# A linear-attention and mixture-of-experts kernel: bonus sums in the output's own columns, an earlier state copy, and routing rows copied a chunk later

## The chip, the core and the metric

The kernel runs on one core of one Trainium2 chip. The metric is the device time of one execution in microseconds (us); lower is better. The core's engines work side by side, each through its own list of instructions in a fixed order: PE (TensorE, the matrix engine; its weight loads are shown as PEld), DVE (VectorE), ACT (ScalarE), POOL (GpSimd) and SP (SyncE, which here only issues transfers). They wait for each other through semaphores. PSUM is the memory into which PE writes its products, in banks; SBUF is the large on-chip memory.

## What is computed

Two layers, one after the other. The first is a linear attention with a decaying state, over 4 batches, 8 heads, 768 tokens and a head size of 48:

```python
for t in range(S):
    cur = einsum('bhd,bhe->bhde', u[None] * k[t], v[t])     # the bonus: only for the token itself
    y[:, :, t] = einsum('bhd,bhde->bhe', r[t], state + cur)
    state = w[t][..., None] * state + einsum('bhd,bhe->bhde', k[t], v[t])
```

The second takes y as 3072 tokens x 384 and runs a mixture of experts: a token with `x @ w_skip > 0` goes to the one of 8 experts with the largest `x @ w_gate` and becomes `x + gate * relu(x @ w1[e]) @ w2[e]` (inner size 1024); the others stay as they are.

## The kernel before

The order of the work is written out by hand: each engine gets its instructions in the order in which the program's text issues them, and no scheduler moves them.

**Chunks.** The attention is cut into 24 chunks of 128 tokens (6 for each of 4 batches). For each chunk the decays are turned into running products by scans, so that a chunk becomes a few matrix products. A tile of a chunk has the 8 heads as 4 pairs (index `a`), with the two heads of a pair in the lower and the upper half of the partitions (index `g`).

**The loop.** A loop over `s` from -2 to 24 (L654 to L726) works at several chunks at once. Step `s` does, in the order of the text:

- SP: the loads of chunk s+4 (`wrk`, L164, and the transposed values `vt`) and of the values `vN` of chunk s+3 (L176); in step -2 also a table of constants and the routing weights `wgp_sb` (L172, four transfers). Then, in step -2, ACT copies the odd pairs' routing weights to `wgo_sb` (L665, L666).
- `store(s-1)`: ACT copies the routing logits and the tokens of the chunk before out of PSUM (L471, L474), SP stores them.
- `update(s)`: PE adds k times v of the chunk to the state, which stays in PSUM in the bank `psu` (L415). In the last chunk of a batch DVE zeroes it instead.
- `drip`: one or more routing steps on DVE. When a group of chunks is through, its gates, ranks and one-hot places are worked out by a list of some 25 short steps (they all show line L238, the helper that issues them), which this call hands out one or two at a time between the attention's own steps. Ranks and places are summed by PE in the same PSUM bank as the state.
- `prep_scan(s+2)`: the first scan `q` on DVE (L333), from the products `p` of neighbouring decays, which POOL has made (L317).
- `outputs(s)`: PE adds masked scores times values (L441) and the read of the state copy `sblk` (L447) to y, in the two PSUM banks `psY` (`yb`).
- `prep_keys(s+2)`: POOL scales the keys (`kq`, L349), DVE runs the second scan (L351). `products(s+3)`: POOL makes `p`, `rk` = r times k, and one more (L317, L319, L326).
- `drip` twice; then `prep_reads(s+2)`: DVE scales the reads (`rp`, L356).
- `carry(s)`: DVE decays the state in PSUM (L424). `evict(s)`: ACT copies y to SBUF (`xT`, L453).
- `prep_check(s+2)`: ACT's range check (L364) and a small copy (L366), the last readers of the chunk's `wrk` but for POOL.
- `quadratic(s+1)`: PE's scores (L374), DVE's two masks (L390), then `bonus_sums`: PE sums r u k over each head (L398) into the upper 256 columns of each `psY` bank, and two matmuls of zeros (`warm`, L401) that add nothing to the lower 256 columns, in which y is to be summed; then `keys`: PE transposes the scaled keys (L383) and ACT copies them out (`kt`, L385); then `bonus`: DVE multiplies the sums by the values and writes the product to y's lower columns (L405), to which `outputs` adds in the next step.
- DVE's part of a weight split (L702), `drip` again.
- `carry_out(s)`: ACT copies the decayed state to `sblk` (L433). `rows_out(s)`: PE multiplies `xT` with the routing weights (L461), `wgp_sb` for even pairs and `wgo_sb` for odd ones.
- `flush`: work that the routing has held back for ACT and PE. From step 2 on the weights of the first two experts are loaded and split into high and low halves too, on ACT, POOL and DVE.

**The experts.** Behind the loop the routed tokens are gathered, run through two layers of PE products and scattered. The first expert's tokens come from a gather that starts when all chunks but the last are routed.

A matmul's `start` flag clears what its columns held before; without it the product is added. `QUARTERS` lists the four (`a`, `g`) quarters of each bank with the even `a` first.

## Time and profile before

| | |
|---|---|
| time, median of 3 runs | 314.21 us (312.47 to 315.76) |
| the profiled execution, its own time | 314.95 us |
| its span, first to last instruction | 313.2 us |
| PE busy | 283.3 us (90%) |
| DVE busy | 225.4 us (72%) |
| ACT busy | 157.3 us (50%) |
| POOL busy | 155.3 us (50%) |
| mean granted clock of PE | 0.966 |

The profile has views of one execution: windows give each engine's busy time, PE's granted clock (1.00 is its full speed) and the transfers of a stretch; the timeline gives single instructions in order of time, with the idle time of the engine ahead of them and what ended it; the chain of waits follows the work that ended last back from the end. `psu<-psu,q` means: written psu, read psu and q. A queue's rows (SPq) are its issues, not the transfers themselves. Busy times of an engine's whole span are means over stretches with different limits, so they are read by stretch below.

### The profile page before, as it was taken

The page shows a single profiled execution, that of the slowest core. Times are in us where ns is not written, and L with a number is a line of the kernel's source. Part 1 is how long each engine was busy: PE and PEld are TensorE (multiplying, and loading weights), DVE is VectorE, ACT ScalarE, POOL GpSimd, SP SyncE. Part 2 cuts the span into 40 slices and gives each one's busy share as a digit, 9 for nine tenths or more (in the row PEclk, how much of TensorE's full clock was granted, in tenths as well). Part 3 has the DMA queues.
Part 4 walks back from the last instruction along what each step waited for, and adds up shares of the span by engine and source line. Part 5 has one row for each costly group of instructions (what it writes and reads, how often), then busy time and mean ns, then how long its engine had stood idle before and what let it go on. Part 6 is the DMA issues. An engine that isn't in the chain of part 4 may idle for free.

```text
span 313.2 us, 9163 instructions
## 1 busy us (share of the span) xinstructions
PE 283.3 (90%) x3642; PEld 260.0 (83%) x3642; DVE 225.4 (72%) x482; ACT 157.3 (50%) x419; POOL 155.3 (50%) x157
## 2 busy tenths in 40 slices
PE   8629999699899799989788999999999999999992
PEld 3328888688788688778688899999999999999992
DVE  5755979979999999998435579496785859496320
ACT  2035555448956478649122458184664828184200
POOL 4976998678998879973103314231222222101111
PEclk9978999879999999999969999999999999999999
DMA  6949999999999998863121196847576474750001
GB/s 149 246 111 256 233 285 245 259 285 295 255 284 277 299 258 224 217 214 96 30 72 40 63 287 246 274 174 251 222 253 235 166 265 157 244 170 27 6 2 39
DMA packets 25604, 60.37 MB, mean 193 GB/s; under 512 B 4326, under 2 KB 15562, under 8 KB 25552
## 3 DMA queue, kind: packets, MB, share of 16 engines
q1 hardware_dynamic: 23184, 53.70, 59.4%
q0 software_dynamic: 2048, 5.48, 5.6%
q10 hardware_dynamic: 320, 0.53, 0.8%
q8 instruction: 30, 0.49, 0.7%
q14 instruction: 22, 0.18, 0.2%
HBM read 52.64 MB, written 7.86 MB: 193 GB/s over the span
## 4 chain that ended last, share of the span: by engine, by line
PE 73%; DMA 9%; ACT 5%; issue 5%; DVE 5%; POOL 1%; POOLq 0%; DVEq 0%; ACTq 0%; SPq 0%
PE psO L860 7%; PE psO L862 7%; PE psO L861 7%; PE psH L839 6%; PE psH L838 6%; PE psH L837 6%; PE psY L441 6%; PE psA L374 5%; PE psH L128 4%; PE psY L398 3%; PE psX L461 3%; PE psY L447 3%; PE psu L415 3%; DMA vt<-wrk 3%; PE psY L401 2%
## 5 line engine op out<-in xcount | busy, mean ns | idle before, releaser
L801 POOL DMA_INDIRECT out<-fin,ids x16 | 16.8, 1051 | 79.3 <-DVE fin L867 44.5
L844 ACT ACTIVATE hh<-psH 128x256 fp32r<-128x256 f32 x60 | 23.1, 384 | 57.9 <-PE psH L839 53.8
L839 PE MATMUL psH<-xTh,w1l 128*128 128x256 f32 x168 | 47.5, 283 | 0.0
L838 PE MATMUL psH<-xTl,w1h 128*128 128x256 f32 x168 | 47.5, 283 | 0.0
L837 PE MATMUL psH<-xTh,w1h 128*128 128x256 f32 x168 | 47.5, 283 | 0.0
L860 PE MATMUL psO<-w2h,hh 128*128 128x384 f32 x120 | 40.8, 340 | 0.0
L862 PE MATMUL psO<-w2h,hl 128*128 128x384 f32 x120 | 40.2, 335 | 0.0
L861 PE MATMUL psO<-w2l,hh 128*128 128x384 f32 x120 | 40.1, 334 | 0.0
L326 POOL TENSOR_TENSOR wrk<-wrk 128x512 f32<-128x512 f32 x24 | 36.5, 1521 | 1.8
L736 POOL DMA_INDIRECT xg<-out,idr x15 | 17.1, 1140 | 40.2 <-DMA out<-fin,ids 25.1
L390 DVE TENSOR_TENSOR asb<-psA,c_sb 128x512 f32<-128x512 f32 x48 | 30.8, 682 | 7.8 <-PE psA L374 7.5
L845 DVE SCALAR_TENSOR_TENSOR hl<-psH,hh 128x256 fp32r<-128x256 f32 x60 | 25.2, 420 | 13.3 <-ACT hh L844 13.0
L349 POOL TENSOR_TENSOR kq<-wrk,q 128x512 f32<-128x512 f32 x24 | 26.9, 1119 | 11.3 <-DVE q L333 10.9
L839 PEld LDWEIGHTS psH<-xTh,w1l 128*128 128x128 f32 x168 | 32.2, 192 | 0.0
L838 PEld LDWEIGHTS psH<-xTl,w1h 128*128 128x128 f32 x168 | 32.2, 192 | 0.0
L837 PEld LDWEIGHTS psH<-xTh,w1h 128*128 128x128 f32 x168 | 32.2, 191 | 0.0
L867 DVE SCALAR_TENSOR_TENSOR fin<-psO,gates,xg 128x384 f32<-128x384 f32 x15 | 9.3, 618 | 28.5 <-PE psO L862 28.5
L441 PE MATMUL psY<-asb,vN 128*64 128x128 f32 (+1 forms) x384 | 27.6, 290 | 2.2 <-DVE psY L405 2.2
L374 PE MATMUL psA<-rp,kq 64*64 64x128 f32 (+1 forms) x768 | 27.5, 261 | 2.2 <-POOL kq L349 2.2
L319 POOL TENSOR_TENSOR rk<-wrk 128x512 f32<-128x512 f32 x23 | 29.3, 1274 | 0.0
L98 DVE TENSOR_TENSOR w2l<-r,w2h 128x512 fp32r<-128x512 f32 x42 | 27.8, 687 | 1.0
L453 ACT COPY xT<-psY 128x512 f32<-128x512 f32 x24 | 14.0, 582 | 27.7 <-PE psY L447 20.2
(155 smaller groups left out, 686.9 us busy)
## 6 DMA issues: line engine op xcount, KB each, us to landing
r<-w SPq DMA_DIRECT2D x48, 512.0 KB, 5.8
wrk<-wrk SPq DMA_DIRECT2D x23, 577.9 KB, 8.1
vN<-vN SPq DMA_DIRECT2D x24, 192.0 KB, 4.7
out<-x SPq DMA_DIRECT2D x24, 192.0 KB, 5.8
vt<-wrk SPq DMA_DIRECT2D x24, 96.0 KB, 5.7
vt<-wrk SPq DMA_DIRECT2D x48, 48.0 KB, 5.3
out<-fin,ids POOLq DMA_INDIRECT x16, 4.7
xg<-out,idr POOLq DMA_INDIRECT x15, 3.9
```

What stands on the lines that cost most here:

```text
L98: (eng or nc.vector).tensor_tensor(dst_l, src, dst_h.bitcast(F32), op=ALU.subtract)
L319: (nc.gpsimd if i else nc.vector).tensor_tensor(rk.rearrange("p a j -> p (a j)"), t[:, R_OFF:K_OFF], t[:, K_OFF:V_OFF], op=ALU.mult)
L326: nc.gpsimd.tensor_tensor(rk1, rk1, two(1, 1, CW), op=ALU.mult)
L374: nc.tensor.matmul(psa[g][j:j + HP, a, j:], wk["kq"][rows, a, j:j + HP], wk["rp"][rows, a, j:], start=True, stop=True)
L390: nc.vector.tensor_tensor(s, psa[g], tri.rearrange("p (o j) -> p o j", o=1).to_broadcast([P, NP, P]), op=ALU.mult)
L441: nc.tensor.matmul(quarter(0, a, g, w), head(i, 2 * a + g, w), wk["asb"][g][:, a], start=False, stop=(c == 0), skip_group_check=True)
L837: nc.tensor.matmul(ps, w1h[:, o:o + P], xTh[:, kc], start=(kc == 0), stop=False)
L838: nc.tensor.matmul(ps, w1h[:, o:o + P], xTl[:, kc], start=False, stop=False)
L839: nc.tensor.matmul(ps, w1l[:, o:o + P], xTh[:, kc], start=False, stop=(kc == KC - 1))
L860: nc.tensor.matmul(pso, h[j, fc][0], w2h[:, o], start=(fc == 0), stop=False)
L861: nc.tensor.matmul(pso, h[j, fc][0], w2l[:, o], start=False, stop=False)
L862: nc.tensor.matmul(pso, h[j, fc][1], w2h[:, o], start=False, stop=(fc == FC - 1))
```

## The change

Three things are edited.

1. `bonus_sums` writes into y's own 256 columns of each bank, not into the upper ones, and `bonus` multiplies there in place. Only the matmuls with an even `a` carry the `start` flag. The two zero matmuls (L401) go. `keys` is issued ahead of `bonus_sums`.
2. `carry` and `carry_out` are issued directly behind `prep_keys` and `products`: on DVE the decay stands ahead of the two routing steps and of `rp`, and on ACT the state copy stands ahead of the eviction and the check.
3. The two copies into `wgo_sb` are issued in step 0 behind `quadratic(1)`, not in step -2.

```diff
--- before.py
+++ after.py
@@ -285,8 +285,8 @@
             scores(i)
             mask(i, 0)
             mask(i, 1)
+            keys(i)
             bonus_sums(i)
-            keys(i)
             bonus(i)
 
         later, held, rare = deque(), [], []
@@ -395,14 +395,11 @@
         def bonus_sums(i):
             for a, g in QUARTERS:
                 rows = slice(64 * g, 64 * g + HP)
-                nc.tensor.matmul(quarter(2 * P, a, g, HP), ubk_sb[rows, a], work[i]["rk"][rows, a],
-                                 start=True, stop=True, skip_group_check=True)
-            for h in range(2):
-                nc.tensor.matmul(yb[:, h, :2 * P], warm[:, :P], warm[:, :2 * P],
-                                 start=False, stop=True, skip_group_check=True)
+                nc.tensor.matmul(quarter(0, a, g, HP), ubk_sb[rows, a], work[i]["rk"][rows, a],
+                                 start=(a % 2 == 0), stop=True, skip_group_check=True)
 
         def bonus(i):
-            nc.vector.tensor_tensor(yb[:, :, :2 * P], yb[:, :, 2 * P:],
+            nc.vector.tensor_tensor(yb[:, :, :2 * P], yb[:, :, :2 * P],
                                     ab(vt_sb[i % (NBUF + 1)]), op=ALU.mult)
 
         def update(i):
@@ -662,8 +659,6 @@
                     for h in range(2):
                         hs = slice(2 * h, 2 * h + 2)
                         halves(nc.sync, wgp_sb[:, hs], wgp[:, hs], swap=bool(h))
-                    nc.scalar.copy(wgo_sb[:, :, E + 1:], wgp_sb[:, 1::2, :2 * D])
-                    nc.scalar.copy(wgo_sb[:, :, :E + 1], wgp_sb[:, 1::2, 2 * D:])
                 if s == -1:
                     nc.sync.dma_start(wgs_sb, wgs)
                 if on(s - 1):
@@ -688,10 +683,13 @@
                     prep_keys(s + 2)
                     if on(s + 3):
                         products(s + 3)
+                if on(s):
+                    carry(s)
+                    carry_out(s)
+                if on(s + 2):
                     drip(2 * pace[0])
                     prep_reads(s + 2)
                 if on(s):
-                    carry(s)
                     evict(s)
                 if on(s + 2):
                     prep_check(s + 2)
@@ -701,10 +699,11 @@
                     if lows and s % 2:
                         nc.vector.tensor_tensor(*lows.pop(0), op=ALU.subtract)
                     drip(2 * pace[0])
-                if on(s):
-                    carry_out(s)
                 if s == n - 1:
                     early_tokens(0)
+                if s == 0:
+                    nc.scalar.copy(wgo_sb[:, :, E + 1:], wgp_sb[:, 1::2, :2 * D])
+                    nc.scalar.copy(wgo_sb[:, :, :E + 1], wgp_sb[:, 1::2, 2 * D:])
                 if on(s):
                     rows_out(s)
                 flush()
```

**ACT, at the program's start.** The kernel before, from the copy of the bonus vector on (`junk` with `wrk` is the range check, `kt` the key copy, `xT` the eviction, `sblk` the state copy):

```order
L267 COPY ubk_sb<-u_sb 128x256
L665 COPY wgo_sb<-wgp_sb 128x2x96
L666 COPY wgo_sb<-wgp_sb 128x2x9
L364 ACTIVATE junk_233,viol<-wrk_82,bias_lo 128x512
L366 COPY q0all<-q_220 128x4
L385 COPY kt_280<-psT_275 128x512
L364 ACTIVATE junk_294,viol<-wrk_83,bias_lo 128x512
L366 COPY q0all<-q_243 128x4
L453 COPY xT_332<-psY 128x512
L364 ACTIVATE junk_334,viol<-wrk_84,bias_lo 128x512
```

The changed kernel, from the same place:

```order
L267 COPY ubk_sb<-u_sb 128x256
L364 ACTIVATE junk_231,viol<-wrk_82,bias_lo 128x512
L366 COPY q0all<-q_218 128x4
L385 COPY kt_268<-psT_263 128x512
L364 ACTIVATE junk_290,viol<-wrk_83,bias_lo 128x512
L366 COPY q0all<-q_241 128x4
L430 COPY sblk_117<-psu 128x4x48
L450 COPY xT_329<-psY 128x512
L364 ACTIVATE junk_331,viol<-wrk_84,bias_lo 128x512
L366 COPY q0all<-q_306 128x4
L385 COPY kt_359<-psT_354 128x512
L705 COPY wgo_sb<-wgp_sb 128x2x96
```

The two routing-row copies have moved from ahead of the first check to behind the second key copy, and the first state copy stands ahead of the first eviction, where it came three instructions later.

**PE, in an early chunk**, from the bonus sums to the routing rows (`rk` against `ubk_sb` are the bonus sums, `kq` the key transposes). Before:

```order
L398 MATMUL psY<-rk_289,ubk_sb 64x128 x8
L401 LDWEIGHTS warm
L401 MATMUL psY<-warm 128x256
L401 LDWEIGHTS warm
L401 MATMUL psY<-warm 128x256
L383 MATMUL psT_465<-c_sb,kq_321 128x128 x4
L461 MATMUL psX_474<-wgp_sb,xT_430 128x105
```

And now:

```order
L383 MATMUL psT_452<-c_sb,kq_317 128x128 x4
L398 MATMUL psY<-rk_285,ubk_sb 64x128 x8
L458 MATMUL psX_468<-wgp_sb,xT_427 128x105
L458 MATMUL psX_468<-wgo_sb,xT_427 128x105
L458 MATMUL psX_468<-wgp_sb,xT_427 128x105
```

The key transposes have moved ahead of the bonus sums, and the two zero matmuls with their weight loads are gone.

**DVE, in one later chunk with routing steps** (L238; `oh` is a one-hot compare, `MEMSET psu` zeroes the ranks' columns of the state's bank), from the first scan to the masks. Before:

```order
L333 SCALAR_TENSOR_TENSOR q_1633<-p_1543,pss 128x260
L346 RECIPROCAL p_1543<-q_1633 128x4
L351 SCALAR_TENSOR_TENSOR pss<-p_1543,pss 128x260
L238 TENSOR_TENSOR oh_1660<-key,pss 128x48
L238 MEMSET psu 128x48
L356 TENSOR_TENSOR rp_1663<-wrk_82,pss 128x512
L424 TENSOR_TENSOR psu<-psu,q_1529 128x4x48
L390 TENSOR_TENSOR asb_14_1687<-psA_114,c_sb 128x512
```

And now:

```order
L333 SCALAR_TENSOR_TENSOR q_1605<-p_1517,pss 128x260
L346 RECIPROCAL p_1517<-q_1605 128x4
L351 SCALAR_TENSOR_TENSOR pss<-p_1517,pss 128x260
L421 TENSOR_TENSOR psu<-psu,q_1503 128x4x48
L238 TENSOR_TENSOR oh_1634<-key,pss 128x48
L238 MEMSET psu 128x48
L356 TENSOR_TENSOR rp_1637<-wrk_82,pss 128x512
L390 TENSOR_TENSOR asb_14_1660<-psA_114,c_sb 128x512
```

The decay of the state (L424 before, L421 now) has moved from behind `rp` to directly behind the second scan, ahead of both routing steps.

## Rows read from the trace of the kernel before

**Rows 1.** Windows: stretch, length, busy us (count) PE, PEld, DVE, ACT, POOL; PE clock, DMA share, GB/s.

```profile
20.50:46.60 26.10, 25.32 (x512) 22.56 (x516) 20.05 (x38) 13.53 (x44) 20.75 (x21) 0.90 0.96 248
46.60:141.00 94.40, 85.04 (x1721) 74.18 (x1714) 87.51 (x190) 59.21 (x180) 80.58 (x74) 0.96 0.96 259
...
200.00:250.00 50.00, 50.00 (x363) 50.00 (x363) 36.81 (x69) 29.95 (x66) 12.90 (x12) 1.00 0.63 213
```

**Rows 2.** Timeline, start of ACT and PE: start, duration, engine, line, op, [idle before, releaser].

```profile
19.39 0.35 ACT L665 COPY wgo_sb<-wgp_sb 128x192 f32<-128x192 f32 x1 [11.59 <-DMA wgp_sb<-wgp]
...
19.76 0.72 ACT L364 ACTIVATE junk<-wrk,bias_lo 128x512 bf16<-128x512 f32 x1
...
20.56 0.58 ACT L385 COPY kt<-psT 128x512 f32<-128x512 f32 x1
...
21.19 1.09 PE L415 MATMUL psu<-vN,kt 128*64 128x48 f32 x16 [6.20 <-ACT kt L385]
```

**Rows 3.** Timeline, from the start to the second eviction: SP, POOL, DVE, PE, ACT.

```profile
13.26 3.07 SPq L172 DMA_DIRECT2D wgp_sb<-wgp  x4
...
17.19 0.62 POOL L317 TENSOR_TENSOR p<-wrk 128x260 f32<-128x260 f32 x1
...
20.64 0.31 SPq L164 DMA_DIRECT2D wrk<-wrk  x1
20.76 0.69 DVE L333 TENSOR_TENSOR_SCAN q<-p,pss 128x260 f32<-128x260 f32 x1 [3.41 <-ACT q0all L366]
...
21.70 0.70 DVE L351 TENSOR_TENSOR_SCAN pss<-p,pss 128x260 f32<-128x260 f32 x1
...
25.77 0.62 POOL L317 TENSOR_TENSOR p<-wrk 128x260 f32<-128x260 f32 x1 [3.02 <-DMA wrk<-wrk]
...
26.93 0.37 PE L461 MATMUL psX<-wgp_sb,xT 128*128 128x105 f32 x2
...
30.20 0.59 ACT L453 COPY xT<-psY 128x512 f32<-128x512 f32 x1 [1.58 <-PE psY L447]
```

**Rows 4.** Windows on either side of two falls of PE's clock.

```profile
57.50:60.00 2.50, 0.47 (x6) 0.30 (x6) 2.34 (x7) 0.69 (x4) 2.50 (x3) 0.98 1.07 286
60.00:61.30 1.30, 0.96 (x17) 0.80 (x18) 1.30 (x4) 0.97 (x4) 1.22 (x2) 0.50 1.04 207
...
21.20:25.80 4.60, 4.60 (x72) 4.27 (x76) 2.10 (x5) 2.13 (x7) 1.15 (x2) 0.51 0.97 241
12.20:19.00 6.80, 2.29 (x54) 1.87 (x54) 3.96 (x7) 0.00 (x0) 6.64 (x7) 0.99 0.72 168
```

**Rows 5.** Chain of waits, one early chunk: start, us, engine, tile, line.

```profile
38.35 0.67 PE psu L415 x16
...
41.87 0.33 PE psY L401 x2
...
43.53 0.67 PE psu L415 x16
```

**Rows 6.** Timeline of the same early chunk, DVE and ACT.

```profile
38.98 0.70 DVE L351 TENSOR_TENSOR_SCAN pss<-p,pss 128x260 f32<-128x260 f32 x1
...
39.77 0.69 DVE L356 TENSOR_TENSOR rp<-wrk,pss 128x512 f32<-128x512 f32 x1
...
40.38 0.36 DVE L424 TENSOR_TENSOR psu<-psu,q 128x192 f32<-128x192 f32 x1
...
43.16 0.32 ACT L433 COPY sblk<-psu 128x192 f32<-128x192 f32 x1
```

**Rows 7.** Timeline of loaded chunks: waits of DVE, ACT and PE.

```profile
66.60 1.29 DVE L390 TENSOR_TENSOR asb<-psA,c_sb 128x512 f32<-128x512 f32 x2 [1.56 <-PE psA L374]
...
108.11 0.32 ACT L433 COPY sblk<-psu 128x192 f32<-128x192 f32 x1 [2.06 <-DVE rnk L238]
...
108.48 0.67 PE L415 MATMUL psu<-vN,kt 128*64 128x48 f32 x16 [2.18 <-ACT sblk L433]
...
111.56 1.29 DVE L390 TENSOR_TENSOR asb<-psA,c_sb 128x512 f32<-128x512 f32 x2 [0.40 <-PE psA L374]
```

## The prediction

> **What bounds the kernel now.** I read the windows first, to see which engine is full in which stretch, then the timeline of the start, of one early chunk and of the chunks where an engine sat idle over a releaser, and the chain of waits for what one chunk costs on PE. Three regimes come out. In the expert phase PE is busy 50.00 of 50.00 us [rows 1], and nothing of the change is in it, so it can only move earlier as a block. In the early chunks (20.5 to 46.6) PE is busy 25.32 of 26.10 us, DVE 20.05: PE sets the pace. In the loaded chunks (46.6 to 141), where weight splits and routing steps are added, DVE is busy 87.51 of 94.40 us [rows 1]: all its idle time is 6.9 us, the ceiling for any gain there that comes from order alone.
>
> The start is a wait by itself. ACT stands 11.59 us in front of the routing-row copy (L665), whose input lands at about 19.3; behind it in ACT's order are the check of chunk 0 (L364) and the copy of chunk 0's keys (L385), and PE, free since 14.99, waits 6.20 us for the latter [rows 2].
>
> **The start, part by part.** With L665 and L666 gone from the front, the keys (done by 14.99) are copied by 14.99 + 0.58 = 15.6, and PE's first state update is 5.5 us earlier than its 21.19 [rows 2]. That much doesn't last, because the decay and the state copy now stand ahead of the eviction on ACT. For chunk 0: p of chunk 2 ends at 17.19 + 0.62 = 17.8; from q to the end of the second scan takes 22.40 - 20.76 = 1.64, so 19.5 [rows 3]; decay 0.36 and state copy 0.32 [rows 6]: 20.2; eviction 0.59 [rows 3]: 20.8; the check 0.80 (19.76 to 20.56), the next key copy 0.58 and the two routing-row copies 0.37 (19.39 to 19.76) [rows 2]: 22.6. Only then can PE run the routing rows of chunk 0 to their end, which it began at 26.93 [rows 3]: 4.3 us earlier, and the second eviction with them (30.20 becomes 25.9). The load of chunk 3 must keep up: it went out at 20.64 and landed 5.13 later, at 25.77 [rows 3]. Its release on ACT is the check of chunk 0, no longer held; ahead of it on SP stand the four issues that end at 13.26 + 3.07 = 16.3 [rows 3]. It has to go out by about 17.7 (25.9 less 0.4 for copy and hand-over, 0.36, 1.64, 0.7 for p and hand-over, 5.13), so it just does.
>
> Against this stands PE's clock. It was granted 0.99 until 19.0 and half (1.2 of 2.4 GHz) until 25.8; in the stretch before the fall PE was busy 2.29 of 6.80 us, and before the later fall at 60.0 it was busy 0.47 of 2.50 [rows 4]. The 30.20 already contains 4.60 us of PE work at half rate, about 2.3 us. In the changed kernel PE still idles from the keys of chunk 1 (about 18.9) until 20.8, and again until about 22.6, so I expect a fall once more, now over a stretch that is nearly all work: a loss of 1.9 us (if it begins in that idle time) to 3.4 (half of 6.8). I take 3.0. **Start: 4.3 - 3.0 = 1.3 saved**, bounds 0.9 and 4.3.
>
> **The zero matmuls.** Two of 128x256 a chunk, 48 in all, go; the chain of waits puts them at 0.33 us [rows 5]. In the early chunks, 5.18 apart (38.35 to 43.53) [rows 5], the state copy ended at 43.16 + 0.32 [rows 6], just ahead of the next update at 43.53: PE and ACT are tied there, and removing the matmuls alone would gain little more than the tie allows. The new order unties them: the copy moves up, the keys stand ahead of the sums, and the eviction, which the sums now wait for as before, is covered by scores and keys. So 0.33 for three chunks until DVE takes over: **1.0 saved**, bounds 0.3 (one chunk) and 1.7 (five). In the loaded chunks it is idle time of PE, worth nothing by itself.
>
> **The decay ahead of rp.** No instruction is added or removed on DVE. Now rp waits for the scan just before it: start to start 0.79 (38.98 to 39.77), where the decay follows rp after 0.61 (39.77 to 40.38) [rows 6]. With the decay between them the 0.18 is covered; I take 0.15 for the 8 of 14 loaded chunks with a decay where no routing step already fills it: **1.2 saved**, bounds 0 and 2.5 (0.18 for all 14). The early state copy also ends waits such as ACT's 2.06 us for a routing step, after which PE waited 2.18 and DVE 0.40 for the scores [rows 7]: of these only DVE's 0.4 is time. **0.4 saved**, bounds 0 and 1. New on DVE is that a routing memset of the bank stands two places behind the decay in one chunk and waits there for ACT's copy, with rp, masks and the bonus product queued behind it and PE's outputs waiting for those: **0.3 lost** (0.32 plus hand-over, less one short step), bound 1.
>
> What hides the later eviction: the decay waits for DVE's scan, so in loaded chunks the eviction comes up to 1.3 us later than PE is done. Scan to sums' end is 0.6 + 0.36 + 0.32 + 0.59 + 0.67, 2.5 us; DVE's own way from the scan to the bonus product is decay, rp and two masks, 0.6 + 0.3 + 0.6 + 1.2 = 2.7 [rows 6, 7] (0.67 taken as for the update [rows 5]). It fits by 0.2. Without that margin, every chunk pays the excess.
>
> Last, PE idles 0.33 us more in each loaded chunk, and a fall of its clock there costs DVE a wait like the 1.56 us for scores at 66.60 [rows 7], with hand-overs 1.9. I charge a fifth of one: **0.4 lost**.
>
> **Sum**: 1.3 + 1.0 + 1.2 + 0.4 - 0.3 - 0.4 = 3.2 us. The profiled execution took 314.95 us (313.2 of span, 1.75 around it) and gives 311.75; it lies 0.74 above the median of the runs, 314.21, from which I count: **311.0**. A measurement here tells about 1% (3.1 us) from no change.
>
> **A rule weighed.** The 2.06 us in [rows 7] is ACT waiting for a DVE step that only reads the bank it reads itself. The Trainium skill (PSUM — Partial Sum Buffer, PSUM bank collisions raise a hardware error) says that any two engines on one bank and quadrant must be kept apart, reads against reads included; the trace agrees. By the rule alone the waits would only turn round: the routing steps that touch the bank (four memsets and four rank products) would wait for the copy.
>
> **Rivals.**
> - *No fall at the start.* PE keeps full rate: 3.0 more, 308.0. For it: two idle stretches with work between them are not one of 6.20. Against it: the fall at 60.0 followed 2.0 us of idle PE. Chance 0.14.
> - *More falls later.* PE loses the filler and its clock falls once or twice more between 70 and 141, each 1.9: 312.9 to 314.8, taken as 313.5. PE was idle 9.4 of 94.4 us there [rows 1] and would be idle some 15. The Trainium skill (TensorE: Matmul & The Clock Gate, Part 1) calls the throttled state the default, which activity releases; the falls in [rows 4] agree. Chance 0.18.
> - *Waits turned round.* All eight routing steps, not one, pay 0.3 behind the copy: 311.0 + 7 x 0.3 = 313.1. This is what the rule on banks would do here; the order shows only one so close. Chance 0.06.
> - *Transfers keep the lead.* Queues were busy 0.96 over the loaded chunks at 259 GB/s [rows 1]; if loads and not DVE set the pace there, the 1.3 and 1.0 are given back: 313.3. Against it, DVE's 93%. Chance 0.08.
> - *Slower: the eviction behind the decay.* If in loaded chunks ACT reaches the state copy late (it also holds one-hot rows and weight casts), sums and bonus product come late, DVE waits and every chunk lengthens. Below 0.2 us a chunk nothing happens; above it 14 chunks pay: from 0.65 us of delay, (0.65 - 0.2) x 14 = 6.3, it is slower by over 1%: 317.4. Chance 0.07.
> - The forecast, 309.5 to 312.5 by itself: 0.47.
>
> Faster by over 1% (under 311.07): half of the forecast's 0.47, the 0.14 of the first rival, and little of the rest (0.04): 0.42. Slower: 0.07. Within 1%: 0.51. The range leaves out the far half of the first rival, below 307.5, and the last one: 307.5 to 314.5.
>
> **What would show it.** Right: ACT's key copy near 15, PE's first update before 16, the second eviction near 26 (full clock) or near 28 (half); early chunks 4.85 apart; state copy directly after the decay, no wait of it for a routing step. Wrong: evictions that wait for the state copy while DVE waits for the sums; a new half-clock stretch between 70 and 141; p waiting for loads. If the start alone gives more than 3 us, the fall was mis-sized.

## The result and the profile after

The changed kernel takes 311.83 us (median of 20 runs, 309.92 to 315.20) where the kernel before takes 315.74 (20 runs); the ratio is 0.9892, with a 95% interval from 0.9859 to 0.9925. That is 3.4 us less by the ratio. The forecast was 3.2 us less and 311.0 us. Executions of one kernel differ by 2 to 3%, and a profile shows one execution; so times of the whole are taken from the ratios below, and the profiles tell where they come from. A ratio compares those runs of each kernel that lie within 1.5% of its fastest, which are 19 of the changed kernel's 20, but only 2 of 12 for E6 below and 3 of 6 for E12.

The profiled execution of the changed kernel has a span of 308.5 us, 4.7 less than before. The first two windows of [rows 1], of the changed kernel:

```profile
20.50:46.60 26.10, 25.09 (x484) 21.36 (x488) 21.21 (x41) 13.80 (x45) 23.00 (x22) 0.93 0.99 260
46.60:141.00 94.40, 84.18 (x1703) 71.02 (x1695) 87.60 (x192) 60.72 (x181) 81.19 (x75) 0.98 0.93 249
```

The regimes are what they were: DVE is busy 87.60 of 94.40 us in the loaded chunks, where it was 87.51. No sum of busy times shows a gain. The gain shows when the same points of the program are set side by side (starts in the two profiled executions; the gather is the first expert's, on POOL):

| stretch | before | after | difference | forecast |
|---|---|---|---|---|
| start to the second eviction | 30.20 | 26.75 | -3.45 | -1.3 |
| second to sixth eviction (chunks 1 to 5) | 20.11 | 20.17 | +0.06 | -1.0 |
| sixth eviction to the gather's issue | 104.28 | 104.89 | +0.61 | -0.9 |
| gather's issue to the end | 158.57 | 156.72 | -1.9 | 0 |

So the total came out as forecast, and no line of the sum did. Both columns are one execution each, and the one of before is not a firm base: E2 and E3 below, in which the routing-row copies stand where they stood before, have their second eviction at 28.34 and 29.38, with PE's clock falling at 16.5 and 18.2 and not at 18.9. At most 0.7 us of E2's 1.9 are its own zero matmuls of two chunks. The experiments ask where the gain comes from.

ACT in the changed kernel, timeline of the start, to set beside [rows 2, 3]:

```profile
14.19 0.58 ACT L385 COPY kt<-psT 128x512 f32<-128x512 f32 x1 [5.04 <-PE psT L383]
...
19.60 0.32 ACT L430 COPY sblk<-psu 128x192 f32<-128x192 f32 x1 [4.03 <-DVE psu L421]
19.81 0.59 ACT L450 COPY xT<-psY 128x512 f32<-128x512 f32 x1
...
21.57 0.37 ACT L705 COPY wgo_sb<-wgp_sb 128x192 f32<-128x192 f32 x1
...
26.75 0.58 ACT L450 COPY xT<-psY 128x512 f32<-128x512 f32 x1 [1.56 <-PE psY L444]
```

The wait of 11.59 us for the routing rows is gone and the keys are copied at 14.19. ACT's wait is now 4.03 us for DVE's decay, and the first eviction, whose input PE had long finished, stands behind it.

PE of the changed kernel, from chunk 0's outputs to the routing rows, timeline and then windows (columns as in [rows 1]):

```profile
18.29 0.66 PE L383 MATMUL psT<-c_sb,kq 128*128 128x128 f32 x4
20.46 0.67 PE L398 MATMUL psY<-rk,ubk_sb 64*64 64x128 f32 x16 [1.51 <-ACT xT L450]
...
22.10 0.47 PE L458 MATMUL psX<-wgo_sb,xT 128*128 128x105 f32 x2 [0.58 <-ACT wgo_sb L706]
```

```profile
18.95:20.40 1.45, 0.00 (x0) 0.00 (x0) 0.56 (x2) 0.80 (x3) 1.42 (x1) 1.00 0.80 185
...
22.10:22.60 0.50, 0.50 (x4) 0.50 (x5) 0.50 (x2) 0.00 (x0) 0.50 (x2) 0.88 1.04 358
...
23.30:25.70 2.40, 2.40 (x31) 2.37 (x32) 2.08 (x5) 0.94 (x4) 2.24 (x3) 0.50 1.09 248
```

PE waits 1.51 us for the eviction and 0.58 for the routing rows, as forecast; its clock stays at 1.00 through the first wait and falls only at about 22.5. The half-rate stretch covers 3.2 us of work, not 6.8.

### The profile page after: what moved, and what is told of

It is laid out like the page before. It is cut to its first block, busy times and chain, and to the rows that moved or that the text cites. A ratio compares the mean times of both kernels' runs of the same rounds, so it can differ in the third digit from the quotient of the medians.

```text
span 308.5 us, 9037 instructions
## 1 busy us (share of the span) xinstructions
PE 281.7 (91%) x3594; PEld 254.1 (82%) x3594; DVE 225.3 (73%) x482; ACT 157.8 (51%) x419; POOL 155.8 (50%) x157
## 4 chain that ended last, share of the span: by engine, by line
PE 68%; DVE 13%; issue 6%; DMA 4%; POOL 3%; ACT 3%; POOLq 0%; DVEq 0%; ACTq 0%; SPq 0%
PE psO L861 7%; PE psO L859 7%; PE psO L860 7%; PE psH L838 7%; PE psH L837 7%; PE psH L836 7%; PE psY L438 4%; PE psX L458 4%; PE psA L374 4%; PE psY L398 4%; PE psH L128 3%; PE psY L444 2%; PE psT L383 2%; PE psu L412 2%; DVE q L333 2%
## 5 line engine op out<-in xcount | busy, mean ns | idle before, releaser
L735 POOL DMA_INDIRECT xg<-out,idr x15 | 16.4, 1096 | 36.0 <-DMA out<-fin,ids 22.4
L349 POOL TENSOR_TENSOR kq<-wrk,q 128x512 f32<-128x512 f32 x24 | 26.9, 1119 | 11.6 <-DVE q L333 10.3
L374 PE MATMUL psA<-rp,kq 64*64 64x128 f32 (+1 forms) x768 | 25.9, 251 | 3.3 <-POOL kq L349 1.9
L98 DVE TENSOR_TENSOR w1l<-r,w1h 128x512 fp32r<-128x512 f32 x36 | 24.9, 693 | 2.1
```

What stands on the lines that cost most here:

```text
L98: (eng or nc.vector).tensor_tensor(dst_l, src, dst_h.bitcast(F32), op=ALU.subtract)
L374: nc.tensor.matmul(psa[g][j:j + HP, a, j:], wk["kq"][rows, a, j:j + HP], wk["rp"][rows, a, j:], start=True, stop=True)
```

## The experiments

In the table, "second eviction" and "lead" (how much earlier than in the kernel before chunk 5 is evicted) come from the profiled execution. So do the next four columns, for the stretch of the loaded chunks from chunk 7's first scan to chunk 23's second mask: its length, DVE's busy time in it (overlaps counted once), what DVE's six weight-split subtractions took (five of them lie in that stretch in E5), and DVE's idle time, which is the rest. The last column is how long POOL's product `p` waited for a chunk's load between 46.6 and 141 us of the same execution.

| kernel | ratio to before (95%) | second eviction | lead | loaded | DVE busy | splits | DVE idle | POOL waits for loads |
|---|---|---|---|---|---|---|---|---|
| before | 1 | 30.20 | 0 | 104.0 | 94.0 | 6.95 | 10.0 | 0.5 |
| after | 0.989 (0.986 to 0.993) | 26.75 | 3.4 | 104.6 | 94.2 | 7.11 | 10.5 | 3.0 |
| E1 copies alone | 0.992 (0.987 to 0.997) | 25.49 | 4.45 | 104.05 | 94.1 | 7.07 | 9.9 | 0.2 |
| E2 bonus sums alone | 1.005 (1.001 to 1.010) | 28.34 | 1.7 | 106.9 | 95.5 | 7.99 | 11.5 | 8.1 |
| E3 early carry alone | 1.007 (1.003 to 1.011) | 29.38 | 1.1 | 106.5 | 95.9 | 8.61 | 10.7 | 0 |
| E4 after, sums first | 1.003 (0.998 to 1.008) | 28.54 | 2.3 | 106.6 | 96.8 | 9.43 | 9.8 | 6.1 |
| E5 after, splits ahead of the scan | 0.985 (0.977 to 0.993) | 25.42 | 4.7 | 103.9 | 91.95 | 4.02 | 12.0 | 0 |
| E6 after, eviction first | 0.984 (0.976 to 0.993) | 25.75 | 3.8 | 108.05 | 96.7 | 8.94 | 11.4 | 4.8 |
| E7 after, splits on POOL | 0.988 (0.981 to 0.996) | 26.98 | 3.2 | 101.8 | 86.7 | none | 15.1 | 0.9 |
| E8 = E4 + E6 + E7 | 0.986 (0.981 to 0.991) | 26.46 | 4.1 | 104.2 | 87.9 | none | 16.3 | 2.5 |
| E9 after, zeros at the start | 0.989 (0.982 to 0.996) | 25.57 | 3.7 | 106.6 | 95.0 | 8.27 | 11.6 | 6.9 |
| E10 = E8 + E9 | 0.990 (0.985 to 0.995) | 24.76 | 5.0 | 106.8 | 87.5 | none | 19.3 | 5.0 |
| E11 = E1 + splits on POOL | 0.997 (0.992 to 1.003) | 26.80 | 2.7 | 107.1 | 89.1 | none | 18.0 | 3.5 |
| E12 = E4 + E6, splits a step later | 0.980 (0.972 to 0.989) | 24.84 | 3.3 | 107.5 | 93.5 | 8.03 | 14.0 | 8.6 |

### E1: the routing-row copies alone

```diff
 # the kernel before; in step -2, behind the loads of wgp_sb
-                    nc.scalar.copy(wgo_sb[:, :, E + 1:], wgp_sb[:, 1::2, :2 * D])
-                    nc.scalar.copy(wgo_sb[:, :, :E + 1], wgp_sb[:, 1::2, 2 * D:])
 # in step 0, ahead of rows_out
+                    nc.scalar.copy(wgo_sb[:, :, E + 1:], wgp_sb[:, 1::2, :2 * D])
+                    nc.scalar.copy(wgo_sb[:, :, :E + 1], wgp_sb[:, 1::2, 2 * D:])
```

> The kernel before with part 3 alone: the two routing-row copies (L665, L666 of before) behind quadratic(1) in step 0, all else as before. Theory (nearly all that the change gains is gained at the start): the key copy near 14.2 us, the first update near 14.8, the second eviction at 26.8 us or earlier, since here the first eviction stands ahead of the decay and not behind it; later chunks keep that lead, and the ratio to the kernel before is 0.986 to 0.990. Rival (the prediction's own sum: the start is worth 1.3 us and the other two parts the rest): ratio 0.995 to 0.997.

ACT's timeline of the start:

```profile
15.02 0.58 ACT L385 COPY kt<-psT 128x512 f32<-128x512 f32 x1 [5.66 <-PE psT L383]
...
17.26 0.59 ACT L453 COPY xT<-psY 128x512 f32<-128x512 f32 x1 [0.86 <-PE psY L441]
...
25.49 0.58 ACT L453 COPY xT<-psY 128x512 f32<-128x512 f32 x1 [1.49 <-PE psY L447]
```

The first eviction is at 17.26 where the changed kernel has 19.81, and the second at 25.49. Behind that, each of chunks 3 to 22 is evicted 4.34 to 4.45 us earlier than before: the old schedule, moved as a block. In this execution the copies alone give more than the whole change does. The trace is the theory's; the ratio, 0.992, lies between the theory's range and the rival's, and its interval reaches into both. It can't be told apart from the whole change's 0.989.

### E2 and E4: the zero matmuls and the order of keys and sums

```diff
 # E2: the kernel before
-                nc.tensor.matmul(quarter(2 * P, a, g, HP), ubk_sb[rows, a], work[i]["rk"][rows, a],
-                                 start=True, stop=True, skip_group_check=True)
-            for h in range(2):
-                nc.tensor.matmul(yb[:, h, :2 * P], warm[:, :P], warm[:, :2 * P],
-                                 start=False, stop=True, skip_group_check=True)
+                nc.tensor.matmul(quarter(0, a, g, HP), ubk_sb[rows, a], work[i]["rk"][rows, a],
+                                 start=(a % 2 == 0), stop=True, skip_group_check=True)
...
 # E4: the changed kernel
-            keys(i)
             bonus_sums(i)
+            keys(i)
```

> The kernel before with part 1 alone and with the sums still ahead of the key transposes: bonus sums in y's own columns, one start flag per bank, no zero matmuls, keys behind the sums. Theory (the 0.33 us of the two zero matmuls was eaten by PE's changes between products of 64x64 and of 128x128 weights, each 0.17 us of PE time, of which the new order has two more): with one such change as before, early chunks come 4.85 us apart, where they were 5.18 before and are 5.20 in the changed kernel. Rival (something else holds the early chunks at 5.2, such as POOL, busy 18.63 of 20.10 us there, or sums that write where y is evicted from): 5.1 to 5.2. The start is as before, second eviction near 30.2; total 0.5 to 1.3 us less by the theory, none by the rival.

> The changed kernel with the bonus sums ahead of the key transposes again, as before the change; all else changed. Theory (changes between 64x64 and 128x128 weights cost 0.17 us of PE time each, and the order keys, sums, rows has two more of them): early chunks 4.85 us apart and not 5.20, 1.0 us gained by chunk 5 and kept or lost to DVE's pace later: 0 to 1.2 us under the changed kernel, ratio 0.985 to 0.989 to the kernel before. Rival (the keys stand ahead to cover the wait of the sums for the eviction, so without them PE waits for ACT): a wait of PE at the sums for the eviction of 0.2 us or more in each early chunk, 5.1 to 5.4 apart, ratio 0.989 to 0.995.

What led to them is PE's part in an early chunk, which has no gap in either kernel. The chain of waits, before and then after (start, us, engine, tile, line):

```profile
36.19 0.51 PE psY L398 x16
36.69 0.32 PE psY L401 x2
37.02 0.44 PE psT L383 x4
37.45 0.87 PE psX L461 x8
```

```profile
37.95 0.59 PE psT L383 x4
38.54 0.60 PE psY L398 x16
39.14 1.07 PE psX L458 x8
40.21 0.60 PE psu L412 x16
```

Sums, zeros, keys and rows took 2.14 us; without the zeros, keys, sums and rows take 2.26. The weight loads of the changed kernel (timeline, PEld) say why:

```profile
37.88 0.43 PEld L383 LDWEIGHTS psT<-c_sb,kq 128*128 128x128 f32 x4 [0.17 <-issue]
38.47 0.43 PEld L398 LDWEIGHTS psY<-rk,ubk_sb 64*64 64x64 f32 x16 [0.16 <-ACT junk L364]
39.07 0.30 PEld L458 LDWEIGHTS psX<-wgp_sb,xT 128*128 128x128 f32 x2 [0.17 <-issue]
```

In front of each of them stand 0.16 to 0.17 us in which nothing is waited for that explains it (ACT's check, named in the second row, ended 0.02 us before it, but the same 0.17 us stand in front of the sums at 102.14, where the last check ended 5.7 us earlier), and each is a change between weights of 64x64 and of 128x128. The order scores, sums, zeros, keys, rows had one such change; scores, keys, sums, rows has three. The Trainium skill (TensorEngine Tiling (Array Packing), Tiling Modes) says that a change of the tiling mode drains the engine. The trace agrees, with about 0.17 us a change. With the sums first again, E4's evictions in early chunks (ACT, timeline):

```profile
38.53 0.58 ACT L450 COPY xT<-psY 128x512 f32<-128x512 f32 x1 [0.18 <-PE psY L444]
...
43.45 0.58 ACT L450 COPY xT<-psY 128x512 f32<-128x512 f32 x1
```

They are 4.92 apart, where the changed kernel has 5.20, no wait for the eviction of 0.2 us stands in each chunk, and of the three gaps one is left: the theory holds. E2 has 5.01 to 5.06 up to chunk 4, less than before but not 4.85. A weight load of PE waits there for the late state copy (0.19 us at 36.14), the tie that the prediction had seen.

Yet the total of E4 is 1.003 and that of E2 1.005, where both theories had a gain. What is won in the early chunks is lost in the loaded ones, which E5 to E7 take up. The starts of these two executions were the clock's: in E4 it was at half from 20.8 to 27.6, with the second eviction at 28.54; in E2 it fell early, and the eviction came at 28.34 where its theory had 30.2.

### E3: decay and state copy early, alone

```diff
 # the kernel before, with the order of the changed one
+                    carry(s); carry_out(s)          # behind prep_keys and products
                     drip(2 * pace[0])
                     prep_reads(s + 2)
-                    carry(s)
                     evict(s)
...
-                    carry_out(s)
```

> The kernel before with part 2 alone: decay and state copy directly behind prep_keys and products, ahead of routing steps, rp and eviction. Theory (this part gives nothing in the loaded chunks: DVE was idle 6.9 us there before and is idle 7.3 us in the changed kernel, its waits only stand elsewhere): from the eviction of chunk 5 to the gather's issue within 0.8 us of before's 104.28, ratio 0.998 to 1.003; the eviction of chunk 6, which comes behind the state copy, later by some 3 us and caught up by chunk 7. Rival (the prediction's: 0.9 us saved): ratio 0.997, and 103.4 between the two.

The ratio is 1.007 and the stretch from chunk 5 to the gather 106.9 us: a loss, beyond both theories (and by the windows above DVE is idle 6.8 us in the changed kernel, not the theory's 7.3). Chunk 6 is evicted 7.95 us behind chunk 5, as in the changed kernel, and what the two kernels share there is seen in the changed one (timeline of ACT, then PE):

```profile
54.65 0.32 ACT L430 COPY sblk<-psu 128x192 f32<-128x192 f32 x1 [4.02 <-DVE psu L421]
54.86 0.59 ACT L450 COPY xT<-psY 128x512 f32<-128x512 f32 x1
```

```profile
55.51 0.67 PE L398 MATMUL psY<-rk,ubk_sb 64*64 64x128 f32 x16 [2.45 <-ACT xT L450]
```

DVE is late with the decay, the eviction waits behind the copy and PE waits 2.45 us for it. Between 46.6 and 141 us the changed kernel has seven such waits (in total, times, longest); the kernel before has four of 1.8 us in all:

```profile
PE psY L398 <- ACT xT L450: 7.9, 7, 2.4
```

Behind the wait in chunk 6 PE's clock falls, and DVE waits for PE twice (windows, then DVE's timeline, of the changed kernel):

```profile
56.60:60.00 3.40, 3.40 (x36) 3.21 (x37) 2.57 (x9) 1.40 (x6) 1.85 (x2) 0.50 1.00 288
```

```profile
58.84 0.10 DVE L238 MEMSET psu<- 128x48 f32 x1 [0.69 <-PE psu L412]
...
61.20 0.37 DVE L421 TENSOR_TENSOR psu<-psu,q 128x192 f32<-128x192 f32 x1 [0.76 <-PE psu L510]
```

So the next chunk has not quite caught up: chunk 7 is evicted 2.6 us ahead of the kernel before, where chunk 5 was 3.4 ahead. The kernel before pays for such a fall too, at 59.9 ([rows 4]), with waits of DVE of 0.30 and 1.56 us. In E3 DVE waits 1.58 us at a routing step's memset for PE's state update, its six splits take 8.61 us instead of 6.95, and chunk 7 is 0.3 us behind the kernel before, where chunk 5 was 1.1 ahead.

### E5, E6 and E7: what DVE and POOL do to each other, and the order on ACT

```diff
 # E5: the changed kernel; ahead of the scan of an odd chunk, no longer behind the bonus product
+            if lows and i % 2:
+                nc.vector.tensor_tensor(*lows.pop(0), op=ALU.subtract)
...
 # E6: the changed kernel
-                    carry_out(s)
...
                     evict(s)
+                    carry_out(s)
...
 # E7: the changed kernel; POOL takes a split at every step, DVE none
-            if lows and i % 2 == 0:
+            if lows:
                 nc.gpsimd.tensor_tensor(*lows.pop(0), op=ALU.subtract)
```

> The changed kernel with DVE's six weight-split subtractions (L700) moved from behind the bonus product to directly ahead of the next odd chunk's first scan, where POOL has run out of work or is about to. Theory (a DVE operation with all operands in SBUF stands still while POOL works through an operation of its own, so the loaded chunks are as long as these meetings make them): the six take under 6 us in all, where they take 7.1 us in the changed kernel, 6.95 before and 9.4 with the sums first (0.68 each alone), and the stretch from the eviction of chunk 5 to the gather's issue is 1 to 2 us under the 104.9 us of the changed kernel. Rival (the loaded chunks' length is set by loads or by waits of DVE, not by these meetings): the six get shorter or not, and the stretch stays within 0.7 us of 104.9.

> The changed kernel with the state copy (L430) behind the eviction on ACT again; the decay stays early on DVE. Theory (at the start, and in chunk 6, the first of a batch, the eviction waits for nothing but the decay that stands ahead of the copy): first eviction at 17.3 us and not 19.8, second at 25.5 and not 26.8, chunk 6 evicted 4.5 us behind chunk 5 and not 7.95; lead of about 4.4 us over the kernel before at chunk 5, where the changed kernel has 3.4. In total 0 to 1.5 us under the changed kernel. Rival (the copy ahead of the eviction pays, since the next chunk's state read hangs on it): early chunks more than 5.25 apart, and no gain.

> The changed kernel with the six weight-split subtractions of DVE (L700) given to POOL, ahead of its key product in the odd chunks, as POOL has six in the even ones. Theory (DVE sets the pace of the loaded chunks, 7.1 us of it are these six and more is lost to their meetings with POOL's operations; POOL was busy 81 of 94 us and takes six of 1.3 to 1.7 us): loaded chunks shorter by 2 to 4 us in all until POOL is full too, ratio to the kernel before 0.977 to 0.985. Rival (POOL becomes the bound, or the loads are): loaded chunks as long as in the changed kernel, within 0.7 us, and DVE idle in front of masks or rp.

What lengthens the splits was read from DVE's and POOL's timelines side by side. One split of the kernel before, then one of E4 with what POOL did meanwhile:

```profile
68.40 0.68 DVE L702 TENSOR_TENSOR w2l<-r,w2h 128x512 fp32r<-128x512 f32 x1
```

```profile
122.98 1.98 DVE L700 TENSOR_TENSOR w1l<-r,w1h 128x512 fp32r<-128x512 f32 x1
124.89 0.68 DVE L333 TENSOR_TENSOR_SCAN q<-p,pss 128x260 f32<-128x260 f32 x1
...
122.91 1.51 POOL L326 TENSOR_TENSOR wrk<-wrk 128x512 f32<-128x512 f32 x1
124.49 1.60 POOL L331 TENSOR_TENSOR w1l<-r,w1h 128x512 fp32r<-128x512 f32 x1
```

Alone, the subtraction takes 0.68 us. Started 0.07 us behind one of POOL's products it takes 1.98 and ends 0.5 us behind that product's end, and POOL's next one takes 1.60 where its shortest took 1.26. DVE's other work on 128x512 (masks, bonus product, reads) has an operand in PSUM and stays at 0.67 to 0.72 in all kernels. The pattern holds for all 60 splits that DVE makes in the ten kernels where it makes any: the 51 that started while one of POOL's operations had more than 0.04 us to go ended 0.54 to 0.55 us behind that operation's end, whatever they took (0.73 to 2.04 us); the other nine took 0.68 to 0.69. The Trainium skill (SBUF — State Buffer, Who interferes with whom) says that a DVE instruction with two inputs in SBUF contends with a GpSimd instruction that reads SBUF, for a pair of ports that only one of them can hold; the traces agree, with these 51 and nine. The profile counts such a wait as busy time, which is why "DVE is busy 93%" looked like work.

So what the splits take is set by where they fall among POOL's operations, and every edit ahead of them can shift that. It is not shown that the length of the loaded chunks follows from it. Set against the kernel before, E4's loaded chunks are 2.6 us longer and DVE's busy time there 2.8 us more. But E2's and E9's are 2.9 and 2.6 us longer with only 1.4 and 1.0 us more of DVE's work. There POOL waits for the chunks' loads (waits of POOL, 46.6 to 141, in total, times, longest: before, the changed kernel, E2, E4):

```profile
POOL p L317 <- DMA wrk<-wrk: 0.5, 1, 0.5
POOL p L317 <- DMA wrk<-wrk: 3.0, 2, 2.0
POOL p L317 <- DMA wrk<-wrk: 8.1, 7, 1.8
POOL p L317 <- DMA wrk<-wrk: 6.1, 6, 2.0
```

A POOL that is late for its loads also meets the splits elsewhere, so in E2, E4, E6 and E9 loads and meetings are not told apart. In E3 POOL has no such wait, and the splits are long all the same.

E5 shortens the splits as its theory wanted (five of them 4.02 us). But one split waits 2.0 us for ACT's cast, and the cast had waited for the weights' load (ACT, then DVE, timeline):

```profile
92.14 0.62 ACT L109 CAST w1h<-r 128x512 fp32r<-128x512 f32 x1 [3.58 <-DMA r<-w]
92.80 0.69 DVE L333 TENSOR_TENSOR w1l<-r,w1h 128x512 fp32r<-128x512 f32 x1 [2.00 <-ACT w1h L109]
```

At chunk 12 E5 is 5.6 us ahead of the kernel before, and at chunk 13 only 2.2. From chunk 5's eviction to the gather it takes 105.5 us where 102.9 to 103.9 were expected: the meetings are gone and the time isn't, which is what the rival said. E7 takes the splits away: DVE's busy time falls by 7.5 us and the loaded stretch by 2.85, within the theory's range; the ratio, 0.988, is above it. But all of the 2.85 us is won by the eviction of chunk 7 (59.27, where the changed kernel has 61.82), with one split of 1.54 us gone and no fall of PE's clock in chunk 6. From there to the last mask both kernels take 88.0 to 88.1 us, though DVE has five splits fewer there in E7. So neither test shows that the meetings set the pace; taking them away alone won nothing clear of the noise. The rest of the 7.5 came back as waits of DVE (waits in 46.6 to 141, in total, times, longest), as E7's rival had it:

```profile
DVE rp L356 <- POOL wrk L326: 5.1, 5, 1.2
DVE q L333 <- POOL p L317: 1.1, 3, 0.4
```

E6 does at the start what was expected (first eviction 16.75) but keeps only 0.4 us more of the lead; chunk 6 is 4.58 behind chunk 5. Its loaded chunks are 3.4 us longer, with splits of 8.94 us, 4.8 us of POOL's waits for loads and a half-clock stretch from 136 to 139. Its total is open: 0.984 rests on two runs, and the median of all its 12 is 0.994 of the kernel before's.

### E9: PE kept busy at the start

```diff
 # the changed kernel, keys(i), ahead of the transposes
+                if i == 1:
+                    for _ in range(6):
+                        nc.tensor.matmul(pst.rearrange("p a j -> p (a j)"), warm[:, :P], warm,
+                                         start=True, stop=True)
```

> The changed kernel with six matmuls of zeros (128x512, into the key transposes' PSUM tile before they write it) ahead of chunk 1's key transposes, so that PE works through most of the 1.45 us in which it waits for the first eviction. Theory (PE's clock falls to half at 22.5 us in the changed kernel and stays there to 25.8 because PE stood idle just before; 3.26 us of its work at half rate are 1.6 us): no half-clock stretch before 30 us, second eviction at 25.1 and not 26.75, later chunks keep the lead until DVE sets the pace; in total 0 to 1.6 us under the changed kernel. Rival (the half-clock stretch comes anyway, since PE still waits 0.6 us for the routing-row copies, or because of the load of PE before): the stretch is there, second eviction 26.5 to 27.

The second eviction is at 25.57, near the theory's 25.1. But windows of the start, of E9 and then of E5, whose program is that of the changed kernel up to chunk 5, show that it settles little:

```profile
14.00:16.00 2.00, 2.00 (x28) 1.41 (x29) 1.54 (x4) 1.35 (x4) 1.92 (x2) 0.57 1.09 252
16.00:18.00 2.00, 2.00 (x30) 1.91 (x28) 1.88 (x4) 0.04 (x1) 1.92 (x4) 0.57 0.41 107
18.00:20.00 2.00, 1.97 (x40) 1.28 (x37) 1.84 (x5) 0.00 (x0) 1.92 (x2) 1.00 0.79 206
```

```profile
20.00:22.00 2.00, 1.07 (x18) 0.72 (x18) 1.34 (x3) 2.00 (x7) 1.92 (x3) 1.00 0.95 235
22.00:24.00 2.00, 1.65 (x28) 1.54 (x30) 1.93 (x4) 0.92 (x5) 1.92 (x3) 1.00 0.97 239
24.00:26.00 2.00, 2.00 (x62) 1.80 (x58) 1.64 (x3) 0.90 (x3) 1.92 (x2) 1.00 1.13 276
```

In E9 the clock fell before the zeros, at half rate for most of 14 to 18. In E5 it did not fall at all: second eviction 25.42, where the same instructions gave 26.75 in the changed kernel and 26.98 in E7. E9's ratio is that of the changed kernel. Whether PE's clock falls at the start is a matter of the execution, and it costs 1.3 to 1.6 us.

### E8, E10, E11 and E12: edits together

> The changed kernel with three edits together: state copy behind the eviction on ACT, bonus sums ahead of the key transposes, and DVE's six weight splits given to POOL. Theory (the three costs found so far are independent: about 1 us of lead at the start, 0.3 us in each of four early chunks, and the meetings of DVE's SBUF operations with POOL's): chunk 5 evicted 5.5 us ahead of the kernel before, the stretch from chunk 7's first scan to the last mask at 102 us or less (104.6 in the changed kernel, 101.8 with the splits on POOL alone), ratio to the kernel before 0.972 to 0.980. Rival (once POOL sets the pace, a lead won at the start is given back to it): the lead at chunk 5 is there and gone by chunk 15, ratio 0.983 to 0.988.

> The three edits of the kernel with state copy behind the eviction, sums first and splits on POOL, and the six matmuls of zeros ahead of chunk 1's key transposes too. Theory: as that kernel, with no half-clock stretch at the start, second eviction near 24, chunk 5 evicted 6 to 7 us ahead of the kernel before; ratio 0.968 to 0.980. Rival (the lead is given back in the loaded chunks, which POOL's work then bounds): the same total as that kernel within 0.5 us.

> The kernel before with part 3 alone (the routing-row copies moved) and DVE's six weight splits given to POOL; parts 1 and 2 are not in it. Theory (parts 1 and 2 gave nothing of their own beyond a share of chance in where DVE meets POOL): start as with part 3 alone, chunk 5 evicted 4.45 us ahead, loaded chunks as short as with the splits on POOL in the changed kernel (101.8 from chunk 7's first scan to the last mask, within 1 us), ratio to the kernel before 0.976 to 0.986, no more than 0.5 us from the kernel with all edits but its early chunks. Rival (the early decay and the freed PE are what lets POOL and DVE keep up): 103 or more, ratio 0.988 or more.

> The changed kernel with the state copy behind the eviction on ACT, the bonus sums ahead of the key transposes, and each weight split's subtraction a step later, so that its input from ACT is long there, DVE's six directly ahead of an odd chunk's first scan. Theory (two of the terms that offset each other in the changed kernel are taken away: the early chunks' 0.3 us each, and the splits' meetings with POOL): chunk 5 evicted 4 to 5.5 us ahead of the kernel before; the six splits under 5.2 us in all with no wait for ACT ahead of them; the stretch from chunk 7's first scan to the last mask 101.5 to 103.5 us, where the changed kernel takes 104.6; ratio to the kernel before 0.975 to 0.985. Rival (transfers: their queues are full from 20 to 118 us in every kernel here, and a kernel that runs ahead of them waits for its chunk): the lead grows past 6 us by chunk 9 and falls back below 5.5 by chunk 13, with POOL's product of decays waiting for a load and DVE's scan behind it; ratio 0.983 to 0.990.

E8 has the edits of E4, E6 and E7 together, E10 also that of E9. E11 is E1 with E7's edit, without parts 1 and 2. E12 has E4's and E6's edits, and this one, by which a split waits until two steps behind its cast's issue:

```diff
 # E12; DVE's splits behind the bonus product go
-            if lows and i % 2 == 0:
-                nc.gpsimd.tensor_tensor(*lows.pop(0), op=ALU.subtract)
 # born: the loop's steps in which the casts were issued (its bookkeeping is left out here)
+            if lows and born[0] <= i - 4:
+                born.pop(0)
+                (nc.vector if i % 2 else nc.gpsimd).tensor_tensor(*lows.pop(0), op=ALU.subtract)
```

None has both of its theory's numbers. E10's start went as wanted (no half-clock stretch before 84 us, second eviction at 24.76), but its lead at chunk 5 is 5.0 us and not 6 to 7. E8 is 8.6 us ahead of the kernel before at chunk 9, and 4.2 at chunk 12; E10 9.1 at chunk 8 and 2.3 at chunk 12. POOL's waits in E8's loaded chunks and ACT's timeline there name the cause, and ACT's timeline in E12, where the lead at chunk 4 is 5.5 us and at chunk 5 only 3.3:

```profile
POOL p L317 <- DMA wrk<-wrk: 2.5, 3, 1.1
```

```profile
80.52 0.54 ACT L471 COPY x<-psX 128x192 f32<-128x192 f32 x2 [3.13 <-DMA out<-x]
...
81.92 0.56 ACT L450 COPY xT<-psY 128x512 f32<-128x512 f32 x1
```

```profile
46.02 0.62 ACT L110 CAST w2h<-r 128x512 fp32r<-128x512 f32 x1 [4.14 <-DMA r<-w]
...
47.03 0.61 ACT L453 COPY xT<-psY 128x512 f32<-128x512 f32 x1
```

A kernel that runs ahead waits for a chunk's load, for the first weights, or for the store of earlier tokens, and in ACT's order the eviction waits behind the cast of those weights or the copy of the tokens. So in E8, E10 and E12 transfers take much of the lead back, as E12's rival said; those of E8 and E10 had put it down to POOL's own work. A large lead is not needed for such waits: E2, E4 and E9, 1.7 to 3.7 us ahead at chunk 5, wait for loads as long or longer. E12 has the lowest ratio, 0.980, but from 3 of 6 runs, which lie between 305.63 and 315.43 us, and its splits (8.03 us) were not shortened as its theory wanted: POOL, itself late for loads, was at work ahead of the odd scans too. Its interval overlaps the changed kernel's; no version here is shown to beat it. In E11 the loaded chunks take 107.1 us and not 101.8: with POOL as full as that, parts 1 and 2 are not without use, which is the rival's side.

## Why the prediction came out right, and where it was wrong

The total is right by luck: the errors of its terms cancel. Step by step:

- **The start, 4.3 saved without the clock.** Right in mechanism and nearly in size: the same program without a fall (E5) has its second eviction at 25.42, 4.8 us earlier, where 25.9 was forecast. ACT's order was followed to the point: the wait for the decay, the eviction at 19.8 and not 20.2, the routing rows behind it. How much of it to expect in other executions is less firm, since the 30.20 it is counted from is one execution (E2 and E3 have 28.34 and 29.38).
- **The clock at the start, 3.0 lost.** This term was mis-sized. It was priced as a fall through the whole stretch of work; the fall came later, at 22.5, and cost 1.3 us (26.75 against 25.42), and in E5 it did not come. The start gave 3.45 and not 1.3. The rival without a fall had the same wrong price of 3.0.
- **The zero matmuls, 1.0 saved.** Wrong: +0.06. The step that failed is that PE's other work would stay as it was. The key transposes went ahead of the sums, and the two more changes between 64x64 and 128x128 weights cost what the zeros had cost. The timeline of the kernel before already had 0.17 us of "issue" in front of the zeros' weight load, which was not weighed.
- **The decay ahead of rp and the early copy, 1.2 + 0.4 - 0.3 - 0.4 saved.** Not borne out: the loaded chunks took 0.6 us longer and not 0.9 shorter, and 2.3 to 2.6 longer with part 1 or part 2 alone, both of which are slower than before. What the two parts are worth on top of part 3 the runs leave open (0.989 against 0.992 with part 3 alone, each known to 0.3 to 0.5%). The step that failed is the first one, that DVE's busy time in the loaded chunks is work of fixed length, so that only its 6.9 us of idle time could move. Between 94.0 and 96.8 us of it were measured from chunk 7's first scan on, in kernels with the same 207 instructions of DVE there (206 in E3).
- **The eviction behind the decay.** The margin of 0.2 us was not the point. It costs the start about 2.5 us at the first eviction (19.81 against 17.26 in E1) and 0 to 1.3 at the second, and in the loaded chunks seven waits of PE, 7.9 us in all, where the kernel before has four of 1.8. DVE went on meanwhile, as argued, but for chunk 6: there PE's wait of 2.45 us is followed by a half-clock stretch and DVE's waits of 0.69 and 0.76. E6, with one such wait of PE left (0.7 us), has no shorter loaded chunks, so these waits alone did not set their length.
- **Behind the gather, nothing.** The profiled execution has 1.9 us there. The clock was at half from 155.5 to 162.3 before and from 152.2 to 155.6 after. Across all kernels here that part takes 156.6 to 159.3 us with the same instructions, so 1.9 us is within that spread, and it is part of why the profiles differ by 4.7 us and the runs by 3.4. The clock alone doesn't order them: E4 takes 156.6 us and E11 158.8, both without a half-clock stretch there until the last 3 us.
- **Rivals.** Transfers keeping the lead had a chance of 0.08. They are not out of it: POOL waits twice for a chunk in the changed kernel, 0.9 us at 102.1 and 2.0 at 108.8, where before it waited 0.5 once. That they set its pace is not shown; they do take lead from E5, E8, E10 and E12. The routing memset behind the decay waits 0.33 us for ACT's copy, once, as forecast; the waits have not turned round as a whole. More falls between 70 and 141: none in the changed kernel, as the window's clock of 0.98 says; 0.96 before.

What stays open: why the three parts together lose 0.6 us in the loaded chunks when each of parts 1 and 2 alone loses over 2. The times of the splits (7.11, 7.99 and 8.61 us), the waits for loads (3.0, 8.1 and 0) and the idle time all differ. Each is read from one profile, and the loaded chunks of E9 are 2.0 us longer than those of the changed kernel with the same program there; so a difference of 2 us between two profiles is not by itself an edit's doing. Half-clock stretches don't settle it either: E4 has none in its loaded chunks and takes 106.6 us.

## What to carry to other kernels

An instruction that waits for a late load at the head of an in-order engine is worth looking for first: moving two copies gave as much as the whole change, as far as the runs can tell. Read the busy time of an engine operation by operation, shortest against mean: where the same subtraction takes 0.68 us here and 1.98 there, the "full" engine is waiting. Gains in a phase where several engines and the transfers are nearly full do not add up: what an edit frees on one of them came back here as waits for another. Before products of another tile shape are moved, count the changes of shape in the new order.

## What was not expected of the hardware

- A change of PE between 64x64 and 128x128 weights cost 0.16 to 0.17 us, with no wait shown but "issue"; two more of them per chunk took back 0.33 us of removed matmuls.
- DVE's subtraction of two SBUF tiles took from 0.68 to 2.04 us (E6), by what POOL did at the time, and the wait is inside its recorded duration. Small steps were stretched as well: a step on 128x6 numbers took 0.90 us in the changed kernel beside a product of POOL, and 0.17 alone (E4, at 136.6).
- The same first 40 us of program ran with PE's clock at full rate in one execution (E5) and with some 3.4 us at half rate in others, from 22.5 us on (the changed kernel) and from 22.8 on (E7); in E9 a fall came at 14.3, ahead of anything that differs. The Trainium skill (TensorE: Matmul & The Clock Gate, Part 1) says that the gate's view of activity is not tied to the kernel's start; the four executions agree.
